# Batch 0's queries and keys loaded by fours, the weights' low parts on one engine, and new issue costs in a planner

## The chip, the cores and the metric

The kernel runs on one core of a Trainium2 chip. A core has a matrix engine (TensorE, PE in the profile), a vector engine (VectorE, DVE), an activation engine (ScalarE, ACT), a general engine (GpSimd, POOL) and a sync engine (SyncE, SP), which here issues every DMA. 16 DMA engines carry out what SP issues. The metric is the time of one execution on the device in microseconds, the median of the runs.

## What is computed

The input is q, k and v of 8 batches, 8 heads, 576 tokens and 64 elements, all float32, and weights of one feed-forward block. Cut to what matters:

```
factor, Sd = 4, S // 4
q_d, k_d, v_d = mean of each 4 tokens of q, k, v           # 144 pooled tokens
out_up    = repeat(softmax(q_d k_d^T / 8) v_d, 4)          # coarse attention
scores    = q k^T / 8, kept where |i - j| < 4              # local attention
out_local = softmax(scores) v
x   = out_up + out_local, heads side by side               # 4608 tokens x 512
xn  = (x - mean) / sqrt(var + 1e-6) * g_ln
out = x + relu(xn @ w_ch1) @ w_ch2                         # 512 -> 2048 -> 512
```

The weights arrive as float64 and are cut to float32 on the chip from their two 32-bit words. Each product of the feed-forward block is made of three matmuls, high by low, low by high and high by high, so each weight and each activation exists as a high part and a low part.

## The kernel before, in words

**The order is planned ahead.** Every step is given to a planner (`Plan`) with an engine, a cost in microseconds, its predecessors, a due time, the buffers that it takes and gives back, and for a DMA a latency (`lag`) and a size (`kb`). The planner walks through time, gives each engine the step that can start first and is due earliest, and the instructions are recorded in that order. On the chip each engine works its list strictly in that order. The costs are used for the order alone. `T0` and `CHUNK` set when the feed-forward chunks are due, `rate` the speed at which the planner lets DMAs land. A step can have a second engine (`alt`), and then the planner takes the one that can start first.

**Stages.** Local attention works in windows of 2 x 58 tokens, five per batch: `local(i)`. Coarse attention works by batch and by half of the heads: `pooled_half`. `norm(n)` joins both for a tile of 128 tokens and normalises it. `ffn(c, p)` is one of eight pairs of hidden blocks for chunk c of 256 tokens; there are 18 chunks. `weights(which, f)` loads one of the 32 blocks of weights and splits it. Chunks 0 and 1 run side by side while the weights come in; from chunk 2 on, all the weights are in the on-chip memory.

**Batch 0 before.** For each of its five windows, `load_rows` (L428) loads q and k with one token in a partition: two DMAs of 64 rows for each, each row in 8 pieces of 256 bytes, one for each head. `turn` (L458) transposes the block on PE with an identity matrix, four transposes of 128 x 128; `turn_out` (L465) copies the result from PSUM by ACT; `sums` (L480) adds four neighbouring tokens on DVE, four instructions for each block, which gives the pooled q and k of batch 0 (`gsum`). The scores (L526) use the turned blocks. The pooled scores of batch 0 (L766) need the sums of all windows. V comes behind q and k in SP's list: for the coarse attention in blocks of 72 rows with four tokens each (L700, `raw0v` and `raw1v`, 1024-byte pieces, added up on POOL at L713 and L714), and for the windows (L443, `vwin`). Behind V stand the first weights (L347, `s`).

**Weights.** ACT makes the high word (L359, `high_word`), DVE shifts and joins the low word (L367 and L370, `low_word`), ACT rounds to the high part (L378, `high`), and the low part is a subtraction (L383, `low`) for which the planner may choose DVE or POOL.

**Other steps named below.** `exps_by_pair` (L566) and `turn_a_out` (L582) are local attention's exponentials and the copy of the turned result; `times_v` (L596) multiplies by v; `turn_a_out` (L795) and `times_v` (L802, `gv`) are the same in the coarse attention; `expand` (L884, L890) joins the two for batch 0 on PE; `move` (L659, L662, `x<-xl`) copies rows of a window's result to the tile they belong to by DMA, at most 58 rows at a time. L197 is a matmul that only keeps PE busy. SP uses eight completion semaphores in turn: a DMA waits until the one eight places ahead of it has landed.

Of the kernel before, what the change touches and what calls it, by code (L numbers as in the profile page):

```python
# [22 lines left out]
class Plan:  # L23
# [3 lines left out]
    def __init__(self, rooms, spare):  # L27


        self.tasks = []  # L30
        self.rooms = rooms
        self.spare = spare
        self.cold = 3
        self.hold = 0.5
        self.lags = (80, 0.3, 0.6)
        self.rate, self.moved = 245.0, 0.0

# [102 lines left out]
def attention_then_ffn(  # L140
# [10 lines left out]
    nc = tc.nc  # L151
# [118 lines left out]

    T0 = 35
    C1 = 5
    CHUNK = 55
    PACE = CHUNK / NPR

# [43 lines left out]
    U, A, STG = (("u", 1),), (("a", 1),), (("stg", 1),)  # L319
    DMA, LAT, W_AHEAD = 0.5, 2.9, 40  # L320
# [16 lines left out]
    def weights(which, f):  # L337
# [42 lines left out]
        def low(eng):  # L380
            x = box[key]
            lo = unit([P, 512], f"lo{name}", F32R)
            eng.tensor_sub(lo, x.a.bitcast(F32), x.hi.bitcast(F32))  # L383
# [18 lines left out]
    chosen, own_moves = {}, []  # L402
    last_local = SimpleNamespace(v=[None] * NVW)

    def local(i):
# [44 lines left out]
        own = b < NPB  # L450
        for src, nm in ((q, "q"), (k, "k")):
            if by_pe:
# [14 lines left out]

                def sums(nm=nm):

                    for par in range(2):  # L470
                        t0 = window_start(w, par)
                        g0, g1 = (-(-(NQ * (2 * w + p)) // FACTOR) for p in (par, par + 1))
                        g1 = min(g1, SD)
                        c0 = 64 * par + FACTOR * g0 - t0
                        p = x.p[nm].rearrange("p (c t) -> p c t", c=NPAIR)
                        for hg in range(2):
                            key = (b, hg, nm)
                            if key not in gsum:
                                gsum[key] = unit([P, 2, SD], f"gs{nm}{b}_{hg}")
                            nc.vector.tensor_reduce(  # L480
                                out=gsum[key][:, :, g0:g1],
                                in_=p[:, 2 * hg : 2 * hg + 2, c0 : c0 + FACTOR * (g1 - g0)]
                                .rearrange("p c (g r) -> p c g r", r=FACTOR),
                                axis=AX.X, op=ALU.add,
                            )
# [4 lines left out]
                if own:  # L490
                    t = add("DVE", 4 * dve(120), sums, [t] + gsum_done.get((b, nm), []), due - 8.0,
                            take=() if w else (("u", 2),))
                    gsum_done.setdefault((b, nm), []).append(t)
                turned.append(add("ACT", act(512), turn_out, (t,), due - 8.0, take=U, give=A))
            else:
# [9 lines left out]
                for jb in range(2):  # L505
                    ts.append(add("SP", 4 * DMA, lambda src=src, nm=nm, jb=jb: load_blocks(src, nm, jb), ts,
                                  due - 14.0, take=() if jb else U, lag=LAT, kb=128, ahead=AHEAD))
                turned.append(add("DVE", dve(512), turn, ts, due - 8.0, take=U, give=U))
        vt = add("SP", 4 * DMA, load_v, (last_local.v[i % NVW],), due - 8.0, lag=LAT, kb=256, ahead=AHEAD)

        def scores_by_pair():

            x.ps = [
                psa(f"ls{i}_{h2}")[:, : NPAIR * 64].rearrange("p (c j) -> p c j", c=NPAIR) for h2 in range(2)
            ]
            for h2 in range(2):
                nc.tensor.matmul(
                    x.ps[h2], lhsT=ident_b, rhs=mask_b.unsqueeze(1).broadcast_to([P, NPAIR, 64]),
                    start=True, stop=False,
                )  # L520
            for pr in range(NPAIR):
                for h2 in range(2):
                    ds = slice(64 * h2, 64 * h2 + 64)
                    for par in range(2):
                        hs = slice(64 * par, 64 * par + 64)
                        nc.tensor.matmul(  # L526
                            x.ps[h2][hs, pr], lhsT=x.qt[ds, pr, hs], rhs=x.kt[ds, pr, hs],
                            start=False, stop=pr == NPAIR - 1,
                        )
# [76 lines left out]
        def divided(h2, eng):  # L606
# [7 lines left out]
            for pr in range(NPAIR):  # L614
# [3 lines left out]
        t = add("PE", 0.75, scores_by_pair if by_pe else scores_by_block, turned, due - 6.0,  # L618
                take=(("a", 2),), give=(("u", 2),))
        if not by_pe:  # L620
# [30 lines left out]
        for e, (n, p0, r0, m, par) in enumerate(moves):  # L651

            def move(n=n, p0=p0, r0=r0, m=m, par=par):
# [7 lines left out]
                for h2 in range(2):  # L661
# [4 lines left out]

            t = add("SP", DMA if by_pe else 2 * DMA, move, outs, due + 1.0, take=() if n in piece else U,
                    give=U if e == len(moves) - 1 else (), lag=LAT, kb=116)
# [13 lines left out]
    def pooled_half(b, hg):  # L682
# [6 lines left out]
        if own:  # L689
            ready["q"], ready["k"] = gsum_done[b, "q"], gsum_done[b, "k"]  # L690
        for nm, src in (("v", v),) if own else (("q", q), ("k", k), ("v", v)):
            for half in range(2):
# [34 lines left out]
    def pooled_pair(b, hg, pr, x, ready):  # L727
# [128 lines left out]
    def norm(n):  # L856
# [259 lines left out]
```

## Time and profile before

| | |
|---|---|
| median of 3 runs | 1064.73 us (1063.45 to 1066.62) |
| the profiled execution's own time | 1069.35 us |
| its span | 1067.0 us |
| busy: PE, DVE, ACT, POOL | 97%, 48%, 29%, 25% |
| DMA | 104.33 MB, mean 98 GB/s |

The profile's busy shares are means over stages that differ. The feed-forward of the first two chunks starts near 62 us, the weights are complete near 162 us, and after that PE is nearly always busy. A start row of the profile tells the time from the span's start, then the duration; "idle before" names what ended a wait. A row of the DMA view is cut into 40 equal slices of its window.

### The profile page before, as it was taken

To read this page: it belongs to the slowest core of one execution; us is meant where nothing else is said; L and a number is where in the kernel's file an instruction comes from. 1 tells how busy PE (TensorE), PEld (TensorE's weight loads), DVE (VectorE), ACT (ScalarE), POOL (GpSimd) and SP (SyncE) were. 2 spreads that over 40 slices of the span, in tenths; PEclk is the share of its full clock that TensorE was granted. 3 is DMA by queue.
4 is the path that set the end of the run, shared out by engine and by line. 5 is a ranking of instruction groups with operands and counts; after the bars stand their busy time and mean duration, and the time that the engine had idled before them with its cause. 6 is when DMAs were issued, how large, how long until landed. Compare 5 with 4: busy or idle time off the path is not lost.

```text
span 1067.0 us, 23720 instructions
## 1 busy us (share of the span) xinstructions
PE 1039.3 (97%) x9280; PEld 932.2 (87%) x9280; DVE 509.5 (48%) x1307; ACT 313.2 (29%) x856; POOL 268.7 (25%) x286
## 2 busy tenths in 40 slices
PE   8897899989999999999999999999989999999998
PEld 8786789979999888889898989898989989888997
DVE  7589954634353534444444443545434454534211
ACT  5575632413332222132222221223222222222110
POOL 4233546323105221231224150142301400000000
PEclk9898999999999999999999999999999999999999
DMA  7788445535433533344354434243442443201000
GB/s 156 214 230 287 129 106 123 146 80 114 88 86 82 119 82 92 69 94 97 77 118 95 106 78 114 42 130 74 109 90 66 87 87 76 62 27 32 9 20 20
DMA packets 289295, 104.33 MB, mean 98 GB/s; under 512 B 237945, under 2 KB 276089, under 8 KB 289185
## 3 DMA queue, kind: packets, MB, share of 16 engines
q1 hardware_dynamic: 289185, 102.83, 40.7%
q8 instruction: 73, 1.20, 0.5%
q14 instruction: 37, 0.30, 0.1%
HBM read 82.58 MB, written 11.80 MB: 88 GB/s over the span
## 4 chain that ended last, share of the span: by engine, by line
PE 87%; DMA 4%; DVE 4%; SPq 2%; ACT 1%; issue 1%; POOL 0%; DVEq 0%; ACTq 0%; POOLq 0%
PE h L996 36%; PE acc L1019 35%; PE gv L802 3%; DMA s<-in_moe_w_ch_dram 3%; PE lv L596 2%; PE gs L766 2%; PE ls L540 2%; PE lt L575 1%; PE px L923 1%; PE gt L785 1%; SPq L428 1%; DVE cva L370 1%; DMA x<-xl 1%; PE gq L739 1%; DVE lo L383 1%
## 5 line engine op out<-in xcount | busy, mean ns | idle before, releaser
L1019 PE MATMUL acc<-hi,hl 128*128 128x512 f32 x576 | 238.2, 413 | 5.3 <-DVE hl L1007 5.3
L1019 PE MATMUL acc<-lo,hh 128*128 128x512 f32 x576 | 228.2, 396 | 0.0
L1019 PE MATMUL acc<-hi,hh 128*128 128x512 f32 x576 | 226.2, 393 | 0.0
L1003 ACT ACTIVATE hh<-h 128x512 fp32r<-128x512 f32 x144 | 86.2, 599 | 437.8 <-PE h L996 393.6
L1007 DVE SCALAR_TENSOR_TENSOR hl<-h,hh 128x512 fp32r<-128x512 f32 x144 | 98.9, 687 | 222.3 <-ACT hh L1003 214.7
L996 PE MATMUL h<-xh,lo 128*128 128x256 f32 x1152 | 193.2, 290 | 0.0
L996 PE MATMUL h<-xlo,hi 128*128 128x256 f32 x1152 | 185.3, 283 | 0.0
L996 PE MATMUL h<-xh,hi 128*128 128x256 f32 x1152 | 185.1, 283 | 0.0
L996 PEld LDWEIGHTS h<-xh,lo 128*128 128x128 f32 x1152 | 168.4, 190 | 16.9 <-POOL lo L383 0.2
L996 PEld LDWEIGHTS h<-xlo,hi 128*128 128x128 f32 x1152 | 159.1, 192 | 0.0
L996 PEld LDWEIGHTS h<-xh,hi 128*128 128x128 f32 x1152 | 158.6, 191 | 0.0
L896 POOL TENSOR_TENSOR x<-x,up 128x512 f32<-128x512 f32 x32 | 41.2, 1289 | 416.6 <-DMA x<-xl 310.9
L1019 PEld LDWEIGHTS acc<-hi,hh 128*128 128x128 f32 x576 | 109.0, 189 | 25.3
L1019 PEld LDWEIGHTS acc<-hi,hl 128*128 128x128 f32 x576 | 109.8, 191 | 22.0 <-DVE hl L1007 6.4
L1019 PEld LDWEIGHTS acc<-lo,hh 128*128 128x128 f32 x576 | 109.9, 191 | 12.5
L930 ACT ACTIVATE xh<-px,gain 128x128 fp32r<-128x128 f32 x144 | 43.6, 372 | 77.1 <-PE px L923 47.7
L940 DVE SCALAR_TENSOR_TENSOR xlo<-px,gain,xh 128x128 fp32r<-128x128 f32 x144 | 42.7, 344 | 34.7 <-ACT xh L930 34.5
L904 DVE BATCH_NORM_STATS2 st<-x 128x6 f32<-128x512 f32 x32 | 21.9, 686 | 47.1 <-POOL x L896 46.0
L779 ACT ACTIVATE ag<-gs,gmx 96x144 f32<-96x144 f32 x96 | 28.9, 373 | 42.9 <-DVE gmx L771 42.7
L1027 DVE SCALAR_TENSOR_TENSOR x<-acc,x 128x512 f32<-128x512 f32 x36 | 24.4, 688 | 35.3 <-PE acc L1019 35.3
L546 DVE TENSOR_TENSOR ls<-ls,mask 128x256 f32<-128x256 f32 x66 | 26.6, 424 | 27.2 <-PE ls L540 27.2
L802 PEld LDWEIGHTS gv<-vd,agt 72*72 72x72 f32 x512 | 37.2, 145 | 1.4
(191 smaller groups left out, 1156.8 us busy)
## 6 DMA issues: line engine op xcount, KB each, us to landing
s<-in_moe_w_ch_dram SPq DMA_DIRECT2D x64, 256.0 KB
vwin<-in_v_dram SPq DMA_DIRECT2D x160, 64.0 KB
out_dram<-x SPq DMA_DIRECT2D x36, 256.0 KB
qr<-in_q_dram SPq DMA_DIRECT2D x264, 32.0 KB
kr<-in_k_dram SPq DMA_DIRECT2D x264, 32.0 KB
up<-ud SPq DMA_DIRECT2D x28, 256.0 KB
x<-xl SPq DMA_DIRECT2D x66, 58.0 KB
ud<-od SPq DMA_DIRECT2D x32, 72.0 KB
```

The lines of the kernel that those rows point to most:

```text
L546: nc.vector.tensor_add(x.ps[n], x.ps[n], mask.unsqueeze(1).broadcast_to([P, NPAIR, 64]))
L779: nc.scalar.activation(y.a[:, c], y.ps[:, c], AF.Exp, scale=POOLED_SCALE, bias=y.mx[:, c : c + 1])
L802: nc.tensor.matmul(y.pv[:, qh, h2], lhsT=y.at[kh][:, h2, qh * GH : (qh + 1) * GH], rhs=vd[:, kh, 2 * pr + h2], start=kh == 0, stop=kh == 1,)
L896: nc.gpsimd.tensor_add(xt[n], xt[n], x.up)
L904: nc.vector.bn_stats(st, x.up if by_pe else xt[n])
L930: nc.scalar.activation(xh[c][i][:, k, j * P : (j + 1) * P], pxt[n][:, kc], AF.Copy, scale=gain[:, kc : kc + 1])
L940: nc.vector.scalar_tensor_tensor(out=xlo[c][i][:, k, ts], in0=pxt[n][:, kc], scalar=gain[:, kc : kc + 1], in1=xh[c][i][:, k, ts].bitcast(F ...
L996: nc.tensor.matmul(ph[c, p][:, fi], lhsT=wt[:, kc], rhs=xx[kc // 2][:, kc % 2], start=n == 0, stop=n == 3 * KC - 1)
L1003: nc.scalar.activation(hh[c, p], ph[c, p], AF.Relu)
L1007: nc.vector.scalar_tensor_tensor(out=hl[c, p].rearrange("p c t -> p (c t)"), in0=ph[c, p].rearrange("p c t -> p (c t)"), scalar=0.0, in1=h ...
L1019: nc.tensor.matmul(acc[c][j], lhsT=lt[:, fi, ts], rhs=rt, start=p == 0 and fi == 0 and n == 0, stop=p == NPR - 1 and fi == 1 and n == 2,)
L1027: nc.vector.scalar_tensor_tensor(out=x, in0=acc[c][j], scalar=1.0 + 2.0**-23, in1=x, op0=ALU.mult, op1=ALU.add)
```

## The change

**Batch 0.** The new `own_half` replaces the loads, turns and sums of batch 0's five windows. The pooled tokens 0 to 73 are half 0, and 71 to 143 are half 1. For each half, each of q and k and each pair of heads there is one DMA (L419) that puts four neighbouring tokens, 1024 contiguous bytes, in a partition: 74 partitions by 2 heads in half 0, 73 by 2 in half 1, 16 DMAs in all where there were 20. PE turns a block with eight matmuls (L428) that each have 64 columns of the block as the stationary operand and the identity as the moving one, and writes each to the place of every fourth token, so the tokens stand in order. DVE adds fours with one instruction for each block (L438), ACT copies out (L445), and the windows' scores (L570) take their 64 tokens from the half that holds them.

**Low parts.** `low` has no second engine any more: all 32 are on DVE.

**Planner.** Costs of SP's steps and of the weights' steps, the latency (2.9 to 2.5, for weights 4.0), `rate` 245 to 260, `T0` 35 to 30 and `CHUNK` 55 to 56.

```diff
-    T0 = 35
+    T0 = 30
     C1 = 5
-    CHUNK = 55
+    CHUNK = 56
...
-        t = add("SP", 2 * DMA, load, (), due, take=(("u", 3),), lag=LAT, kb=512, ahead=W_AHEAD)
-        t = add("ACT", 2 * act(256, True), high_word, (t,), due)
-        t = add("DVE", 0.45 + 2 * dve(256), low_word, (t,), due, give=(("u", 2),))
+        t = add("SP", 1.3, load, (), due, take=(("u", 3),), lag=LAT + W_LAG, kb=512, ahead=W_AHEAD)
+        t = add("ACT", 0.87, high_word, (t,), due)
+        t = add("DVE", 1.26, low_word, (t,), due, give=(("u", 2),))
         t = add("ACT", act(512, True), high, (t,), due, take=U)
-        return add("DVE", dve(512), lambda: low(nc.vector), (t,), due, take=U, give=U,
-                   alt=("POOL", pool(512), lambda: low(nc.gpsimd), 0.3))
+        return add("DVE", 0.69, lambda: low(nc.vector), (t,), due, take=U, give=U)
...
+    own_t, own_done = {}, {}
+    OWN_G = ((0, GH + 2), (GH - 1, SD))
+
+    def own_half(b, half):
+        g0, g1 = OWN_G[half]
+        ng = g1 - g0
...
+            def load(x=x, nm=nm, src=src, pr=pr):
+                x.raw = unit([P, 2, FACTOR, D], f"{nm}o{b}_{pr}_{half}")[:ng]
+                nc.sync.dma_start(
+                    x.raw.rearrange("p h r d -> p h (r d)"),
+                    src[b, 2 * pr : 2 * pr + 2, FACTOR * g0 : FACTOR * g1].rearrange("h (g r) d -> g h (r d)", r=FACTOR),
+                )
+
+            def turn(x=x, nm=nm, pr=pr):
+                x.p = psa(f"l{nm}{b}_{pr}_{half}")[:, : FACTOR * ng].rearrange("p (g r) -> p g r", r=FACTOR)
+                for r in range(FACTOR):
+                    for h2 in range(2):
+                        nc.tensor.matmul(
+                            x.p[64 * h2 : 64 * h2 + 64, :, r], lhsT=x.raw[:, h2, r], rhs=ident[:ng, :ng],
+                            start=True, stop=True,
+                        )
...
-        for src, nm in ((q, "q"), (k, "k")):
+        for src, nm in () if own else ((q, "q"), (k, "k")):
...
-                t = add("SP", 1.46, lambda src=src, nm=nm: load_rows(src, nm), (), due - 12.0, take=U,
-                        lag=LAT, kb=256, ahead=AHEAD)
+                t = add("SP", 1.33, lambda src=src, nm=nm: load_rows(src, nm), (), due - 12.0, take=U,
+                        lag=LAT, kb=360, ahead=AHEAD)
```

**SP, from the last loads of q and k to the first weights.** Before (`qn`, `kn` are q and k of a window, x2 its two halves; `raw0v`, `raw1v` and `vwin` are V; `s` is weights):

```order
L428 DMA qn_272<-in_q_dram 64x8x64 x2
L428 DMA kn_309<-in_k_dram 64x8x64 x2
L700 DMA raw0v_332<-in_v_dram 72x4x256
L700 DMA raw1v_361<-in_v_dram 72x4x256
L443 DMA vwin_76<-in_v_dram 64x4x64 x4
L443 DMA vwin_77<-in_v_dram 64x4x64 x4
L700 DMA raw0v_458<-in_v_dram 72x4x256
L443 DMA vwin_78<-in_v_dram 64x4x64 x4
L700 DMA raw1v_504<-in_v_dram 72x4x256
L443 DMA vwin_79<-in_v_dram 64x4x64 x4
L347 DMA s_0_0_546<-in_moe_w_ch_dram 128x2x256
```

Now, the same stretch with the semaphores that each row waits for (`qo` and `ko` are the new blocks; DMAHW0 to DMAHW7 are the eight completion semaphores):

```order
L419 DMA ko_2_0_164<-in_k_dram 74x2x256 [waits DMAHW0_49]
L419 DMA qo_1_1_179<-in_q_dram 73x2x256 [waits DMAHW1_49]
L419 DMA ko_1_1_194<-in_k_dram 73x2x256 [waits DMAHW2_49]
L419 DMA qo_3_0_208<-in_q_dram 74x2x256 [waits DMAHW3_49]
L419 DMA ko_3_0_222<-in_k_dram 74x2x256 [waits DMAHW4_49]
L419 DMA qo_2_1_236<-in_q_dram 73x2x256 [waits DMAHW5_49]
L419 DMA ko_2_1_248<-in_k_dram 73x2x256 [waits DMAHW6_49]
L419 DMA qo_3_1_267<-in_q_dram 73x2x256 [waits DMAHW7_49]
L419 DMA ko_3_1_282<-in_k_dram 73x2x256 [waits DMAHW0_49]
L746 DMA raw0v_298<-in_v_dram 72x4x256 [waits DMAHW1_49]
L746 DMA raw0v_310<-in_v_dram 72x4x256 [waits DMAHW2_49]
L499 DMA vwin_76<-in_v_dram 64x4x64 [waits DMAHW3_49,DVE_49]
```

V and the weights follow in nearly the same order; the blocks ahead of them have 74 or 73 rows where they had 64.

**DVE, the sums and the windows.** Before, the sums of a window's q and k stand next to the maxima of the window ahead (`gsq`, `gsk` sums, `lmx` maxima of the scores `ls`):

```order
L480 TENSOR_REDUCE gsk_0_178<-lk_206 128x2x14
L480 TENSOR_REDUCE gsk_1_180<-lk_206 128x2x14
L551 TENSOR_REDUCE lmx_252<-ls_0_220 128x4
L551 TENSOR_REDUCE lmx_252<-ls_1_221 128x4
L556 TENSOR_TENSOR ls_0_220<-ls_0_220,lmx_252 128x256
L556 TENSOR_TENSOR ls_1_221<-ls_1_221,lmx_252 128x256
L480 TENSOR_REDUCE gsq_0_158<-lq_244 128x2x15
```

Now:

```order
L438 TENSOR_REDUCE gsk_1_278<-lk_2_1_340 128x72
L438 TENSOR_REDUCE gsq_1_259<-lq_3_1_377 128x72
L438 TENSOR_REDUCE gsk_1_278<-lk_3_1_388 128x72
L595 TENSOR_REDUCE lmx_415<-ls_0_352 128x4
L595 TENSOR_REDUCE lmx_415<-ls_1_353 128x4
L600 TENSOR_TENSOR ls_0_352<-ls_0_352,lmx_415 128x256
L600 TENSOR_TENSOR ls_1_353<-ls_1_353,lmx_415 128x256
L816 TENSOR_REDUCE gmx_0_448<-gs_0_406 96x3
```

All 16 sums stand ahead of the first window's maxima; the last of them is that of `ko_3_1`, the last load.

**POOL, low parts.** Before, a stretch of POOL's list in the weights' stage (`lo` low parts, `raw2q` to `kd` the coarse sums of batch 1):

```order
L383 TENSOR_TENSOR lo_3_1342<-cva_3_956,hi_3_1317 128x512
L713 TENSOR_TENSOR raw2q_1129<-raw2q_1129 72x4x128
L714 TENSOR_TENSOR qd_1371<-raw2q_1129 72x256
L713 TENSOR_TENSOR raw2k_1133<-raw2k_1133 72x4x128
L714 TENSOR_TENSOR kd_1410<-raw2k_1133 72x256
L383 TENSOR_TENSOR lo_4_1438<-cva_4_1182,hi_4_1415 128x512
L383 TENSOR_TENSOR lo_4_1477<-cva_4_1319,hi_4_1464 128x512
```

Now:

```order
L956 TENSOR_TENSOR mv_1059<-mv_1059,neg_half 128x1
L759 TENSOR_TENSOR raw2q_1248<-raw2q_1248 72x4x128
L760 TENSOR_TENSOR qd_1384<-raw2q_1248 72x256
L759 TENSOR_TENSOR raw2k_1261<-raw2k_1261 72x4x128
L760 TENSOR_TENSOR kd_1420<-raw2k_1261 72x256
L759 TENSOR_TENSOR raw2q_1442<-raw2q_1442 72x4x128
L760 TENSOR_TENSOR qd_1384<-raw2q_1442 72x256
```

14 low parts left POOL for DVE; the coarse sums stay.

More of the change, by code (lines that the diff above doesn't have):

```diff
@@ L35, in __init__ @@
         self.lags = (80, 0.3, 0.6)
-        self.rate, self.moved = 245.0, 0.0
+        self.rate, self.moved = 260.0, 0.0
     def add(self, eng, dur, fn, deps=(), due=0.0, take=(), give=(), lag=None, ahead=1e9, alt=None, kb=0):
@@ L319, in attention_then_ffn @@
     U, A, STG = (("u", 1),), (("a", 1),), (("stg", 1),)
-    DMA, LAT, W_AHEAD = 0.5, 2.9, 40
+    DMA, LAT, W_AHEAD, W_LAG = 0.5, 2.5, 40, 1.5
     def act(n, sbuf=False):
@@ L402, in attention_then_ffn, with sums, turn_out @@
     chosen, own_moves = {}, []
-    last_local = SimpleNamespace(v=[None] * NVW)
+    own_t, own_done = {}, {}
[3 more added lines that the diff above has]
+        ng = g1 - g0
+        add = plan.add
+        for e, (nm, src, pr) in enumerate((nm, src, pr) for pr in range(NPAIR) for nm, src in (("q", q), ("k", k))):
+            due = window_at(b * NWIN + (2 * half if half else 0)) - 8.0 + 0.2 * e
+            x = SimpleNamespace()
+            def load(x=x, nm=nm, src=src, pr=pr):
[12 more added lines that the diff above has]
+                        )
+            def sums(x=x, nm=nm, pr=pr):
+                key = (b, pr // 2, nm)
+                if key not in gsum:
+                    gsum[key] = unit([P, 2, SD], f"gs{nm}{b}_{pr // 2}")
+                n0 = half * GH - g0
+                nc.vector.tensor_reduce(
+                    out=gsum[key][:, pr % 2, half * GH : (half + 1) * GH], in_=x.p[:, n0 : n0 + GH], axis=AX.X, op=ALU.add
+                )
+            def turn_out(x=x, nm=nm, pr=pr):
+                t = unit([P, 512], f"o{nm}t{b}_{pr}_{half}")
+                own_t[nm, pr, half] = t
+                nc.scalar.copy(t[:, : FACTOR * ng], x.p.rearrange("p g r -> p (g r)"))
+            t = add("SP", 0.5, load, (), due - 4.0, take=U, lag=LAT, kb=147, ahead=AHEAD)
+            t = add("PE", 0.45, turn, (t,), due, take=A, give=U)
+            done = gsum_done.setdefault((b, pr // 2, nm), [])
+            done.append(add("DVE", dve(288), sums, [t] + done, due + 1.0, take=() if half or pr % 2 else U))
+            own_done.setdefault((b, half), []).append(add("ACT", act(296), turn_out, (t,), due, take=U, give=A))
@@ L405, in local, with own_piece @@
+    def own_piece(nm, pr, w, par, ds):
+        t0 = window_start(w, par)
+        half = int(t0 + 64 > FACTOR * OWN_G[0][1])
+        t0 -= FACTOR * OWN_G[half][0]
+        return own_t[nm, pr, half][ds, t0 : t0 + 64]
+    last_local = SimpleNamespace(v=[None] * NVW, ls=None)
     def local(i):
@@ L466, in turn_out @@
                     setattr(x, nm + "t", t)
[L468 to L485, printed above, removed]
-                t = add("SP", 1.46, lambda src=src, nm=nm: load_rows(src, nm), (), due - 12.0, take=U,
-                        lag=LAT, kb=256, ahead=AHEAD)
+                t = add("SP", 1.33, lambda src=src, nm=nm: load_rows(src, nm), (), due - 12.0, take=U,
+                        lag=LAT, kb=360, ahead=AHEAD)
                 t = add("PE", 0.43, turn, (t,), due - 8.0, take=A, give=U)
[L490 to L493, printed above, removed]
                 turned.append(add("ACT", act(512), turn_out, (t,), due - 8.0, take=U, give=A))
@@ L506, in local @@
                     ts.append(add("SP", 4 * DMA, lambda src=src, nm=nm, jb=jb: load_blocks(src, nm, jb), ts,
-                                  due - 14.0, take=() if jb else U, lag=LAT, kb=128, ahead=AHEAD))
+                                  due - 14.0, take=() if jb else U, lag=LAT, kb=200, ahead=AHEAD))
                 turned.append(add("DVE", dve(512), turn, ts, due - 8.0, take=U, give=U))
-        vt = add("SP", 4 * DMA, load_v, (last_local.v[i % NVW],), due - 8.0, lag=LAT, kb=256, ahead=AHEAD)
+        if own:
+            for half in range(2):
+                if half in {int(window_start(w, par) + 64 > FACTOR * OWN_G[0][1]) for par in range(2)}:
+                    turned += own_done[b, half]
+            turned.append(last_local.ls)
+        vt = add("SP", 2.65 if own else 2.65, load_v, (last_local.v[i % NVW],), due - 8.0, lag=LAT, kb=360, ahead=AHEAD)
         def scores_by_pair():
@@ L520, in scores_by_pair, with of @@
                 )
+            def of(nm, pr, par, ds):
+                if own:
+                    return own_piece(nm, pr, w, par, ds)
+                return getattr(x, nm + "t")[ds, pr, 64 * par : 64 * par + 64]
             for pr in range(NPAIR):
@@ L618, in local @@
         t = add("PE", 0.75, scores_by_pair if by_pe else scores_by_block, turned, due - 6.0,
-                take=(("a", 2),), give=(("u", 2),))
+                take=(("a", 2),), give=() if own and w not in (2, NWIN - 1) else (("u", 2 * NPAIR if own else 2),))
+        if own:
+            last_local.ls = t
         if not by_pe:
@@ L665, in move @@
                     )
-            t = add("SP", DMA if by_pe else 2 * DMA, move, outs, due + 1.0, take=() if n in piece else U,
+            t = add("SP", 0.76 if by_pe else 2.0, move, outs, due + 1.0, take=() if n in piece else U,
                     give=U if e == len(moves) - 1 else (), lag=LAT, kb=116)
@@ L716, in pooled_half @@
                 by_dve = b == 0 and nm == "k"
-                t = add("SP", 0.82, load, (), due - 4.0, take=STG, lag=LAT, kb=288, ahead=AHEAD)
+                t = add("SP", 0.45, load, (), due - 4.0, take=STG, lag=LAT, kb=288, ahead=AHEAD)
                 t = add(
@@ L849, in pooled_pair @@
         od_done.append(t)
-        t = add("SP", DMA, keep, (t,), due, lag=LAT)
+        t = add("SP", 0.42, keep, (t,), due, lag=LAT)
         ud_done.setdefault(b, []).append(t)
@@ L962, in norm @@
         else:
-            t = add("SP", DMA * len(rows), load_up, [d for _, _, b, _ in rows for d in ud_done[b]], due - 4.0,
+            t = add("SP", 0.64 * len(rows), load_up, [d for _, _, b, _ in rows for d in ud_done[b]], due - 4.0,
                     take=U, lag=LAT, kb=256, ahead=12.0)
@@ L1061, in attention_then_ffn @@
     spread_done = plan.add("POOL", 2.5, make_spread, (choice_done,), 20.0, take=U)
+    for b in range(NPB):
+        for half in range(2):
+            own_half(b, half)
     for i in range(NPB * NWIN):
```

4 lines of the change are left out of this document (2 added, 2 removed).

## The prediction

> **What bounds the kernel now.** I read the busy time by stages first, from the page and the view by windows (columns: busy us of PE, weight load, DVE, ACT and POOL, granted clock, DMA share, GB/s).
>
> ```profile
> span 1067.0 us, 23720 instructions
> ...
> 0.00:20.00 20.00, 17.63 (x212) 15.87 (x216) 15.07 (x58) 9.04 (x18) 8.43 (x28) 1.00 0.70 158
> 20.00:40.00 20.00, 19.60 (x317) 17.79 (x318) 13.05 (x49) 15.82 (x55) 7.92 (x8) 1.00 0.73 167
> 40.00:60.00 20.00, 16.80 (x134) 14.04 (x132) 10.69 (x33) 8.87 (x24) 3.48 (x5) 0.83 0.91 265
> 80.00:140.00 60.00, 47.92 (x348) 40.63 (x347) 55.83 (x101) 35.33 (x92) 28.61 (x24) 0.94 0.63 187
> 160.00:1000.00 840.00, 834.20 (x7549) 751.35 (x7549) 374.48 (x981) 212.94 (x588) 203.81 (x208) 1.00 0.39 87
> ```
>
> From 160 us on PE idles 5.8 us in 840: nothing of this change shortens that work, so the end moves by as much as its beginning moves. From 80 to 140 DVE is the fullest engine, 55.83 of 60 us, and PE idles 12.1. Ahead of that lies batch 0's attention, a chain with no second batch to hide behind. What ends last there is seen in SP's list, PE's list and the chain of waits.
>
> ```profile
> 1.31 1.43 SPq L428 DMA_DIRECT2D qn<-in_q_dram  x2
> ...
> 13.63 2.02 SPq L428 DMA_DIRECT2D kn<-in_k_dram  x2
> 15.70 0.64 SPq L700 DMA_DIRECT2D raw0v<-in_v_dram  x1
> ...
> 23.89 2.57 SPq L443 DMA_DIRECT2D vwin<-in_v_dram  x4
> 26.56 0.51 SPq L700 DMA_DIRECT2D raw1v<-in_v_dram  x1
> 27.17 3.05 SPq L443 DMA_DIRECT2D vwin<-in_v_dram  x4
> 30.26 3.27 SPq L347 DMA_DIRECT2D s<-in_moe_w_ch_dram  x4
> ```
>
> ```profile
> 5.50 0.45 PE L458 MATMUL lq<-ident,qn 128*128 128x128 f32 x1 [0.23 <-DMA qn<-in_q_dram]
> ...
> 19.15 0.63 PE L458 MATMUL lk<-ident,kn 128*128 128x128 f32 x4 [0.27 <-DMA kn<-in_k_dram]
> ```
>
> ```profile
> 32.71 4.32 PE gv L802 x64
> ```
>
> The last k is issued by 15.65 and used at 19.15; the coarse attention's product with v follows at 32.71, and the first weights are issued at 30.26 behind all of V. Both start from the moment at which q and k are through. The question is when that is in the changed kernel.
>
> **How many engines a load gets.** The new loads have 74 and 73 rows, so I looked for loads with odd numbers of rows. At 790 us only copies of 58 and 46 rows are in flight (the SP row shows six copies issued back to back; then their sizes, 1 KB a row, the two of 12 rows taken to be through by 791; then three windows).
>
> ```profile
> 786.46 5.95 SPq L662 DMA_DIRECT2D x<-xl  x6
> ```
>
> ```profile
> x<-xl SPq DMA_DIRECT2D x2, 58.0 KB
> x<-xl SPq DMA_DIRECT2D x2, 46.0 KB
> x<-xl SPq DMA_DIRECT2D x2, 12.0 KB
> ```
>
> ```profile
> 791.00:792.00 1.00, 1.00 (x6) 0.76 (x5) 0.91 (x3) 0.00 (x0) 0.00 (x0) 1.00 0.16 36
> 792.00:793.00 1.00, 1.00 (x11) 1.00 (x10) 0.12 (x1) 0.00 (x0) 0.55 (x1) 1.00 0.16 36
> 793.00:794.00 1.00, 1.00 (x10) 0.99 (x9) 0.00 (x0) 0.00 (x0) 0.00 (x0) 1.00 0.16 36
> ```
>
> The share stands still at 0.16 with several copies waiting: 2 of 16 engines are 0.125, and packets that overlap count a little more. So 58 rows (2 x 29) and 46 rows (2 x 23) got two engines each, and the same two, or the share would be higher. A load of 72 rows by 4 heads in pieces of 1024 bytes, alone on the queue:
>
> ```profile
> 621.12 0.31 SPq L700 DMA_DIRECT2D raw12q<-in_q_dram  x1
> ```
>
> ```profile
> DMA  0899100012942345588878987877775412210000
> GB/s 0 36 36 53 53 18 0 36 36 89 71 89 71 107 125 178 196 267 285 303 249 303 321 285 267 303 267 267 267 178 107 89 36 53 53 36 0 0 0 0
> ```
>
> Its plateau is 7 to 8 tenths and mostly 267 GB/s: 12 of 16 engines, and 72 = 12 x 6. All three counts are the largest divisor of the rows that is at most 16. By that pattern 74 = 2 x 37 gets two engines and 73, a prime, one. No row shows a load on one engine; that step is the pattern carried on.
>
> The Trainium skill has it as a rule, in "DMA: Bandwidth & Descriptors", section "Why a DMA increments its semaphore by 16 and not by 1": the count is the largest k up to 16 that divides the slowest dimension of both sides, and a DMA issued from SP takes the lowest-numbered k engines. The trace's 58, 46 and 72 rows agree. By it the one-engine loads also sit on one of the two engines of the 74-row loads.
>
> **The change, part by part.** *Loads.* A 74-row load is 148 pieces of 1024 bytes, 74 on each of two engines; a 73-row load is 146 on one. There are eight of each. With all on the same pair, as the copies above were, the busier engine has 8 x 74 + 8 x 146 = 1760 pieces. Its rate: 267 GB/s over 12 engines is 22.3 GB/s, 46 ns a piece. That is 1760 x 0.046 = 81.0 us. Bounds: the plateau's best slice, 321 / 12 = 26.8 GB/s, gives 38 ns and 67 us; two engines at 36 GB/s, scaled by bytes, 57 ns and 100 us. I take 46, the same size of piece from the same memory. The first DMAs were issued by 2.74 and used at 5.50, 2.8 us, of which some 0.6 is their own transfer. So the last k is used at about 1.3 + 0.4 (one issue; 0.31 to 0.64 in the rows above) + 2.2 + 81.0 = 84.9, against 19.15: 65.8 later.
>
> *What is queued behind.* V and the weights stand behind these loads in SP's list, and each waits for the DMA eight places ahead. Eight DMAs of V are issued while the blocks land and have their share behind them on the busy engine; 13 remain ahead of the first weight, 11 for the windows and two for the coarse attention, which also wait until POOL has added up the first two blocks. 11 x 0.64 (2.57 for four) + 2 x 0.5 = 8.0 us, and some 1.7 for POOL: the weights start at 94.5 instead of 30.26, 64 later. On the compute side every sum stands ahead of the first window's maxima in DVE's list, so four windows and the coarse scores run after 85 one behind the other; the coarse product then ends near 101, against 37, again 64. I take 64 for both.
>
> *Turns.* PE's price for eight matmuls of 64 x 74 is not in the trace. Below: four transposes of 128 x 128 take 0.63, and eight of the 64 x 64 products on all four corners of the array less, by the chain of waits:
>
> ```profile
> 20.00 0.62 PE ls L526 x32
> ```
>
> Above: 64 records of 72 x 65 take 4.32, so 16 for one turn 1.1. At 0.45 (the first transposes' row) to 1.1, sixteen turns are 7 to 18 us, but a load lands every 3.4 to 6.7 us, and that covers all but the last turn. The same cover hides the ACT copies and the sums. If the loads were quick, PE would pay (rivals).
>
> *Low parts.* The rows of the instructions, and one pair on POOL and DVE:
>
> ```profile
> L383 DVE TENSOR_TENSOR lo<-cva,hi x18: 676/684/1359, 71.5 to 161.2; 128x512 fp32r<-128x512 f32 x18
> L383 POOL TENSOR_TENSOR lo<-cva,hi x14: 1275/1296/1558, 47.4 to 124.1; 128x512 fp32r<-128x512 f32 x14
> ...
> L367 DVE TENSOR_SCALAR cva<-cva x32: 410/421/1524, 39.3 to 146.6; 128x512 int32<-128x512 int32 x32
> ```
>
> ```profile
> 100.91 1.55 POOL L383 TENSOR_TENSOR lo<-cva,hi 128x512 fp32r<-128x512 f32 x1 [2.41 <-ACT hi L378]
> ```
>
> ```profile
> 101.23 1.52 DVE L367 TENSOR_SCALAR cva<-cva 128x512 int32<-128x512 int32 x1
> ```
>
> DVE gains 14 x 0.68 = 9.6 us of work in the stage where it is the fullest engine. But beside POOL's 1.55 us the shift took 1.52 instead of 0.42: 1.1 us lost. If each of the 14 costs DVE between 0 and 1.1, the balance is +9.6 to -5.8; most POOL low parts lie in that stage, where DVE is 93% busy, so some 0.6 each is likely, and I take +1. PE's 12.1 us idle in that stage is also the most that the new costs, due times and order of the planner can return; a late weight can cost as much. I take 0, 3 either way.
>
> *Clock.* PE waits some 60 us with only the turns; between 40 and 60, after shorter waits, the granted clock was 0.83, 3.4 us in 20. I add 1 us for a cold restart.
>
> **Sum.** 64 + 1 + 0 + 1 = 66, less 1 for V that has already landed: +65. The profiled execution took 1069.35 and would become 1134. It is 4.6 above the median of the runs, 1064.73, to which the same 65 gives **1130**.
>
> **Rivals.** *One-engine loads elsewhere* (8%): if 73 rows use a third engine, it has 8 x 146 = 1168 pieces, 53.7 us; the last k is used at 57.6, 38 later, and the time is about 1102. For it: no row shows which engine a single one is. Against: the copies all shared one pair.
>
> *Sixteen engines after all* (5%, faster): if pieces are dealt out whatever the rows, 16 loads are 2368 x 0.046 / 16 = 6.8 us. SP's 16 issues then bind at about 0.5 each, and the last k is used near 12, 7 ahead of before, so 1058. It decides from the point where the busiest engine needs no more than before's 15 us: 330 pieces, about 21 a load, seven engines. Against: 116 KB in two copies at 36 GB/s.
>
> *Quick loads, slow turns* (3%, no change): with sixteen engines and turns of 1.1 us, PE is the bound from 4 us on, 16 x 1.1 = 17.6, and q and k are through at 21.6 against 19.8: 1066. The two halves of a block go to different columns of the array, and the row of `ls` shows such columns side by side at 0.62 us for 32 records, so 0.5 is as possible.
>
> **How the numbers follow.** 84% for the forecast. Its own range comes from the piece: 38 to 57 ns are -14 to +19, the other terms 4; without the far ends 1112 to 1144, which leaves the first rival out. Slower by over 0.3% (3.2 us, about what this kernel's runs can tell from none): 92% with the first rival; within: 3%; faster: 5%.
>
> **What would show it.** In the changed profile: DMA share near 0.1 and some 25 to 45 GB/s from 10 to 80 us; SP's `ko` and `qo` rows spread over some 35 us with waits; PE's turns 3.4 and 6.7 us apart, the last near 85; first weights issued near 94; low parts on DVE at 0.68 and the shift near 0.42; PE dense from about 225. Wrong it is if the share is high in the first 15 us, if the last turn comes ahead of 30, or if the stage after the first weights is shorter or longer by more than 5 us than before's.

## The result: 1115.23 us, slower by 50

The changed kernel took 1115.23 us (median of 4 runs, 1114.15 to 1116.16) against 1065.29 for the kernel before (4 runs, 1063.45 to 1066.62); the ratio is 1.0456, with a 95% interval of 1.0434 to 1.0478. The forecast was 1130 in a range of 1112 to 1144: the direction and the cause hold, the size is 15 us too large. The profiled executions span 1112.4 and 1067.0 us, 45.4 apart; the execution of before that was profiled (1069.35) stood 4.1 us above the median of these runs, the changed kernel's 1.1 below.

SP's list in the changed kernel, which answers to the loads of q and k quoted ahead of the result (start, duration):

```profile
1.31 0.40 SPq L419 DMA_DIRECT2D qo<-in_q_dram  x1
1.76 0.45 SPq L419 DMA_DIRECT2D ko<-in_k_dram  x1
2.25 3.24 SPq L419 DMA_DIRECT2D qo<-in_q_dram  x1
5.52 3.30 SPq L419 DMA_DIRECT2D ko<-in_k_dram  x1
...
61.34 6.02 SPq L419 DMA_DIRECT2D ko<-in_k_dram  x1
67.41 7.35 SPq L746 DMA_DIRECT2D raw0v<-in_v_dram  x2
...
89.94 2.14 SPq L347 DMA_DIRECT2D s<-in_moe_w_ch_dram  x4
```

PE's list, with the idle time before each turn in brackets:

```profile
7.75 1.25 PE L428 MATMUL lq<-ident,qo 74*64 74x74 f32 x16 [2.46 <-DMA qo<-in_q_dram]
10.89 1.25 PE L428 MATMUL lk<-ident,ko 74*64 74x74 f32 x16 [1.89 <-DMA ko<-in_k_dram]
...
23.08 1.24 PE L428 MATMUL lq<-ident,qo 73*64 73x73 f32 x16 [4.67 <-DMA qo<-in_q_dram]
29.39 1.24 PE L428 MATMUL lk<-ident,ko 73*64 73x73 f32 x16 [5.07 <-DMA ko<-in_k_dram]
...
80.13 1.24 PE L428 MATMUL lk<-ident,ko 73*64 73x73 f32 x16 [6.04 <-DMA ko<-in_k_dram]
...
97.20 1.38 PE L848 MATMUL gv<-vd,agt 72*72 72x65 f32 x18
98.93 3.20 PE L848 MATMUL gv<-vd,agt 72*72 72x65 f32 x46 [0.35 <-issue]
```

A load of 74 rows adds 3.14 us to the time of its turn and one of 73 rows 6.2 to 6.3 (the last 7.3). With 74 and 146 pieces on the busier engine that is 42 to 43 ns a piece in both. The view of the DMA engines from 5 to 67 us, cut into 40 slices, shows the engines themselves:

```profile
GB/s 48 48 48 48 48 48 48 39 24 24 24 24 37 36 48 48 48 36 24 24 24 24 24 24 31 36 48 43 48 36 24 24 24 24 24 24 24 24 24 24
```

48 GB/s is two engines, 24 is one (1024 bytes in 42.7 ns). Nowhere is it more than 48: no load has a third engine. That holds also from 26.7 to 29.4 us, while a load of 73 rows is still landing (its turn stands at 29.39) and the next one of 74 has begun: a single engine outside the pair would make it 72 there. The trace's records of the completion semaphores agree: as the data of a load of 74 rows land, two increments come, and one for a load of 73 rows (one more stands right behind the issue, at 1.82 us for the first load).

So the last k is used at 80.13 instead of 19.15, the first weights are issued at 89.94 instead of 30.26 (59.7 later), and the coarse product stands at 97.20 instead of 32.71 (64.5 later). From the first weights on the changed kernel is quicker, though. Two windows of each, the 130 us from its first weights and what follows up to 1030 (width, then busy us of PE, weight load, DVE, ACT and POOL, granted clock, DMA share, GB/s), before first, then changed:

```profile
30.30:160.30 130.00, 114.63 (x1029) 99.83 (x1020) 102.96 (x232) 74.33 (x205) 50.87 (x45) 0.95 0.69 194
160.30:1030.00 869.70, 863.90 (x7738) 778.28 (x7737) 381.17 (x996) 218.10 (x601) 203.51 (x208) 1.00 0.38 85
```

```profile
89.90:219.90 130.00, 123.85 (x1184) 111.53 (x1184) 110.40 (x255) 80.35 (x226) 45.72 (x43) 0.97 0.73 205
219.90:1030.00 810.10, 807.46 (x7361) 725.78 (x7362) 374.88 (x971) 207.68 (x567) 188.66 (x194) 1.00 0.39 88
```

PE idles 15.4 us in the first 130 before and 6.2 after the change, then 5.8 and 2.6. That is 12.4 us of the 14.3 by which the span grew less than the first weights moved (59.7 - 45.4). The first product of the feed-forward, before and then changed, moved by nearly the same:

```profile
62.12 0.72 PE L996 MATMUL h<-xh,lo 128*128 128x256 f32 x4
```

```profile
121.35 0.71 PE L1042 MATMUL h<-xh,lo 128*128 128x256 f32 x4
```

It stands 59.2 us later, 5.3 less than the coarse product, and the span from it to the end is 13.8 shorter. So the changed kernel wins time both ahead of the feed-forward and in it. This is the part that the forecast had at 0. The profiled execution of before took 4.1 us more than its median, so these differences of spans are too large by about as much; the runs below give them by medians.

### The profile page after: what moved, and what is told of

Its sections match the earlier page's. It is cut to its first block, busy times and chain, and to the rows that moved or that the text cites. A ratio compares the mean times of both kernels' runs of the same rounds, so it can differ in the third digit from the quotient of the medians.

```text
span 1112.4 us, 23962 instructions
## 1 busy us (share of the span) xinstructions
PE 1043.8 (94%) x9450; PEld 936.5 (84%) x9450; DVE 519.4 (47%) x1300; ACT 311.8 (28%) x850; POOL 250.6 (23%) x272
## 4 chain that ended last, share of the span: by engine, by line
PE 81%; SPq 6%; DVE 5%; DMA 5%; issue 1%; POOL 0%; ACT 0%; DVEq 0%; ACTq 0%; POOLq 0%
PE h L1042 34%; PE acc L1065 33%; SPq L419 5%; PE gv L848 3%; PE gs L812 2%; DMA s<-in_moe_w_ch_dram 2%; PE lv L640 2%; PE ls L584 2%; DMA ko<-in_k_dram 2%; DVE cva L370 2%; PE lt L619 1%; DVE lo L383 1%; PE px L969 1%; PE gt L831 1%; DVE cva L367 1%
## 5 line engine op out<-in xcount | busy, mean ns | idle before, releaser
L1065 PEld LDWEIGHTS acc<-lo,hh 128*128 128x128 f32 x576 | 109.2, 190 | 12.4
L956 POOL TENSOR_TENSOR mv<-mv,neg_half 128x1 f32<-128x1 f32 x36 | 20.0, 556 | 99.4 <-DVE mv L953 78.0
L848 PE MATMUL gv<-vd,agt 72*72 72x65 f32 x512 | 38.2, 228 | 0.3 <-issue 0.3
```

Source lines behind the costliest of these rows:

```text
L848: nc.tensor.matmul(y.pv[:, qh, h2], lhsT=y.at[kh][:, h2, qh * GH : (qh + 1) * GH], rhs=vd[:, kh, 2 * pr + h2], start=kh == 0, stop=kh == 1,)
L1065: nc.tensor.matmul(acc[c][j], lhsT=lt[:, fi, ts], rhs=rt, start=p == 0 and fi == 0 and n == 0, stop=p == NPR - 1 and fi == 1 and n == 2,)
```

## Experiments: the rows of a load

All kernels here differ from the changed kernel in one line; no instruction changes its place, only its number of rows.

```diff
-    OWN_G = ((0, GH + 2), (GH - 1, SD))      # 74 and 73 rows
+    OWN_G = ((0, GH + 8), (GH - 8, SD))      # 80 and 80; GH + 2, GH - 2: 74; + 3, - 3: 75; + 4, - 4: 76
```

**80 and 80 rows.**

> Both halves have 80 pooled tokens (0 to 79 and 64 to 143) instead of 74 and 73; the order of all instructions is the changed kernel's. Theory (the largest divisor of the rows up to 16 sets the engines): 80 rows get 16 engines, the share of the first 15 us is 0.6 or more instead of 0.12, SP issues the 16 loads without a wait in about 7 us, and the turns stand back to back on PE: 16 at the 1.25 us that one took in the changed kernel are 20 us, so the last k is turned near 25 us instead of 81, and the first weights are issued near 24 instead of 89.9. The time falls by 56 to 66 us from 1115: 1049 to 1059. Rival (the rows don't matter, the slow part is the form of the load with four tokens in a partition): the turns stay 3 to 6 us apart and the time stays over 1100.

Measured: 1047.45 us (6 runs, 1043.58 to 1055.76) against 1065.08 for before; ratio 0.9832 (0.9791 to 0.9873). PE's and SP's lists:

```profile
5.21 0.79 PE L428 MATMUL lq<-ident,qo 80*64 80x80 f32 x16
5.84 0.72 PE L428 MATMUL lk<-ident,ko 80*64 80x80 f32 x16
...
16.13 0.72 PE L428 MATMUL lk<-ident,ko 80*64 80x80 f32 x16
...
29.96 4.37 PE L848 MATMUL gv<-vd,agt 72*72 72x65 f32 x64
```

```profile
9.46 0.31 SPq L419 DMA_DIRECT2D ko<-in_k_dram  x1
...
26.73 2.94 SPq L347 DMA_DIRECT2D s<-in_moe_w_ch_dram  x4
```

More bytes, and 68 us less: the rows alone cost that much. The turns were quicker than expected: some 0.6 us apart, so the last is done at 16.9 and not near 25, and the time fell by 2 us more than the range given.

**74 and 74 rows.**

> Both halves have 74 rows (0 to 73 and 70 to 143); nothing else differs from the changed kernel. Theory: all 16 loads get two engines, 148 pieces of 42 ns on two, so a turn every 3.1 us, the last near 5 + 50 = 55 us instead of 80, and about 1090. Rival (the pace of 3.1 and 6.2 us comes from the wait for the eighth DMA back or from something else than the count of engines): the second half's loads still land 6 us apart and the time stays near 1115.

Measured: 1086.03 us (one run). The turns in PE's list:

```profile
7.06 1.25 PE L428 MATMUL lq<-ident,qo 74*64 74x74 f32 x16 [1.78 <-DMA qo<-in_q_dram]
10.21 1.26 PE L428 MATMUL lk<-ident,ko 74*64 74x74 f32 x16 [1.89 <-DMA ko<-in_k_dram]
...
55.34 1.25 PE L428 MATMUL lk<-ident,ko 74*64 74x74 f32 x16 [2.73 <-DMA ko<-in_k_dram]
```

3.14 us apart but for the last two (3.4 and 4.0), the last at 55.3: one more row in the second half saves 29 us. The pace follows the count of engines.

**75 and 75 rows, then 76 and 76.**

> Both halves have 75 rows (0 to 74 and 69 to 143), one row more than the larger half of the changed kernel. Theory: 75 = 5 x 15, so 15 engines, and within 3 us of the 80-row kernel. Rival (any count that isn't a multiple of 16, or an odd one, is slow): like 74 rows or slower, 1090 or more.

> Both halves have 76 rows (0 to 75 and 68 to 143). The largest divisor up to 16 is 4 (76 = 4 x 19): 16 loads of 152 pieces on four engines are 608 pieces each at 42 ns, 25.5 us, a turn every 1.6 us, the last near 31 instead of 16.1 with 80 rows and 80.1 in the changed kernel; about 1061. Rival (more rows are simply better between 74 and 80, as 75 rows look): as fast as 75 rows, under 1054.

Measured: 75 rows 1052.72 us, 76 rows 1063.95 (one run each). In PE's list of the 76-row kernel the turns stand 1.62 us apart, 38 pieces of 42.6 ns on each of four engines:

```profile
7.38 0.75 PE L428 MATMUL lk<-ident,ko 76*64 76x76 f32 x16 [1.01 <-DMA ko<-in_k_dram]
9.00 1.28 PE L428 MATMUL lq<-ident,qo 76*64 76x76 f32 x16 [0.88 <-DMA qo<-in_q_dram]
...
31.70 1.28 PE L428 MATMUL lk<-ident,ko 76*64 76x76 f32 x16 [0.68 <-DMA ko<-in_k_dram]
```

So 74, 75, 76 and 80 rows give 1086, 1053, 1064 and 1047: not by size but by the divisor (2, 15, 4, 16). The Trainium skill states that rule in "DMA: Bandwidth & Descriptors", section "Why a DMA increments its semaphore by 16 and not by 1": the largest divisor of the slowest dimension up to 16, on the lowest-numbered engines. The five counts measured here agree, and so does the one-engine load, which shared an engine with the two-engine ones. For 75 rows, where no spacing shows the count, the completion semaphores do: 15 increments come as a load's data land, 4 with 76 rows and 16 with 80. The one run of the 75-row kernel is 5 us slower than the 80-row one, more than the 3 expected. Its DMAs are not the reason: no turn waits for one, and SP issues the first weights even 1.4 us sooner (25.34 against 26.73). The turns themselves are slow, and so is everything on PE until some 28 us:

```profile
5.21 1.27 PE L428 MATMUL lq<-ident,qo 75*64 75x75 f32 x16
6.26 1.21 PE L428 MATMUL lk<-ident,ko 75*64 75x75 f32 x16
...
22.07 1.22 PE L428 MATMUL lk<-ident,ko 75*64 75x75 f32 x16
23.21 3.20 PE L812 MATMUL gs<-gsk,qbdg 128*96 128x144 f32 x12
...
27.73 1.71 PE L812 MATMUL gs<-gsk,qbdg 128*96 128x144 f32 x12
...
38.43 4.37 PE L848 MATMUL gv<-vd,agt 72*72 72x65 f32 x64
```

```profile
25.34 2.15 SPq L347 DMA_DIRECT2D s<-in_moe_w_ch_dram  x4
```

The two rows of L812 are the same instructions at 3.20 and at 1.71 us: TensorE ran at about half its pace. The coarse product stands at 38.43 instead of 29.96, 8.5 later, and the span is 6.4 longer (1051.0 against 1044.6) although the weights came sooner. So in this pair the chain through the coarse product set the time, not the queue up to the weights.

**75 rows again.**

> The 75-row kernel once more, to see whether its turns stand 1.0 us apart again (the profiled execution had them at 1.21 us each, until 27 us, and the 80-row one at 0.72 to 0.78). Theory (16 turns of 64 columns don't keep TensorE's clock up by themselves; it depends on whether the first matmuls, ahead of them, have brought it up): either pace, and with the quick one 1046 to 1049, with the slow one 1050 to 1054. Rival (15 engines or 75 partitions are slower by themselves): 1052 to 1055 and turns at 1.2 us again with every profile.

Measured: 1049.07 us (4 runs: 1052.83, 1046.88, 1050.20, 1047.94), ratio to before 0.9851 (0.9821 to 0.9882). The profiled execution was the slowest, and its turns were slow again, as in the first profile. All four lie within the range of the 80-row kernel's runs (1043.58 to 1055.76), so the 5 us are not clear of noise. Slow turns go with 1052.7 and 1052.8, but whether the turns of the 1046.88 were quick isn't shown, so neither reading is ruled out.

## Experiments: the low parts and the planner's numbers

The time won outside batch 0's loads has to come from the rest of the change. The first question was which half.

**80 rows, low parts on two engines.** The 80-row kernel, with this in `low`:

```diff
-        return add("DVE", 0.69, lambda: low(nc.vector), (t,), due, take=U, give=U)
+        return add("DVE", 0.69, lambda: low(nc.vector), (t,), due, take=U, give=U,
+                   alt=("POOL", pool(512), lambda: low(nc.gpsimd), 0.3))
```

> 80 rows as in the run above, and the low parts may go to POOL again as in the kernel before. Theory (as in the prediction: what DVE gains by fewer low parts it loses to POOL's port): within 4 us of the 80-row kernel. Rival (the 12 us less idle time on PE after the first weights, 8.8 us instead of 21, came from the low parts on DVE): 8 to 14 us slower than the 80-row kernel.

Measured: 1058.35 us (12 runs), 10.9 more than the 80-row kernel on the same chip. The theory of the prediction falls. Its arithmetic holds: the groups of DVE's weight rows in the 130 us from the first weights, first with POOL, then on DVE alone (count, then busy us and mean ns of one):

```profile
L370 DVE SCALAR_TENSOR_TENSOR cva<-s,cva 128x256 int32<-128x256 int32 x64 | 40.4, 672 | 1.1
L367 DVE TENSOR_SCALAR cva<-cva 128x512 int32<-128x512 int32 x32 | 19.9, 622 | 0.0
L383 DVE TENSOR_TENSOR lo<-cva,hi 128x512 fp32r<-128x512 f32 x17 | 12.6, 748 | 0.0
```

```profile
L370 DVE SCALAR_TENSOR_TENSOR cva<-s,cva 128x256 int32<-128x256 int32 x62 | 33.2, 576 | 1.1
L383 DVE TENSOR_TENSOR lo<-cva,hi 128x512 fp32r<-128x512 f32 x29 | 24.2, 846 | 0.2 <-ACT hi L378 0.2
L367 DVE TENSOR_SCALAR cva<-cva 128x512 int32<-128x512 int32 x31 | 17.1, 550 | 2.1 <-ACT cva L359 2.1
```

12 more low parts on DVE cost 11.6 us there and the other rows gave 10.0 back (three instructions fewer among them): DVE's work is nearly the same, 72.9 and 74.5 us. The 11 us lie elsewhere. Next, the two edits on the kernel before, one at a time and together.

```diff
 before, low parts on DVE
-        return add("DVE", dve(512), lambda: low(nc.vector), (t,), due, take=U, give=U,
-                   alt=("POOL", pool(512), lambda: low(nc.gpsimd), 0.3))
+        return add("DVE", dve(512), lambda: low(nc.vector), (t,), due, take=U, give=U)
 before, new numbers
-        self.rate, self.moved = 245.0, 0.0
+        self.rate, self.moved = 260.0, 0.0
-    T0 = 35
+    T0 = 30
-    CHUNK = 55
+    CHUNK = 56
-    DMA, LAT, W_AHEAD = 0.5, 2.9, 40
+    DMA, LAT, W_AHEAD, W_LAG = 0.5, 2.5, 40, 1.5
...
```

> The kernel before with all low parts on DVE and nothing else. Theory (the 11 us between the two 80-row kernels come from where the low parts run): 8 to 13 us faster than before, 1052 to 1057. Rival (they come only with the planner's new numbers): within 4 us of before.

> The kernel before with the planner's new numbers (T0, CHUNK, rate, latencies, costs of SP's and the weights' steps); loads and low parts as before. Theory (where the low parts run decides): within 4 us of before, 1061 to 1069. Rival (the numbers decide): 8 us or more faster.

> The kernel before with the new numbers and all low parts on DVE: the change without the new loads. In the 80-row kernel the last k is turned 3 us earlier than before and the first weights are issued 3.5 us earlier; if that is what the new loads are worth, this kernel takes 3 to 4 us more than the 80-row kernel's 1047.5, 1050 to 1052. If the new loads are worth nothing it takes 1047; if they carry most of the gain over before (17.6 us), 1058 or more.

> The 80-row kernel (new loads, low parts on DVE) with the planner's numbers of before. Theory (the numbers are worth at most 4 us either way): 1044 to 1052. Rival (the numbers carry the gain): 1056 or more.

| loads of batch 0 | planner's numbers | low parts | us (runs) | ratio to before (95%) |
|---|---|---|---|---|
| as before | old | DVE | 1072.74 (4) | 1.0070 (1.0042 to 1.0098) |
| as before | new | DVE and POOL | 1064.09 (10) | 0.9987 (0.9968 to 1.0006) |
| as before | new | DVE | 1050.61 (4) | 0.9863 (0.9834 to 0.9892) |
| 80 rows | old | DVE | 1074.33 (4) | 1.0109 (1.0053 to 1.0165) |
| 80 rows | new | DVE and POOL | 1058.35 (12) | 0.9937 (0.9911 to 0.9962) |
| 80 rows | new | DVE | 1047.45 (6) | 0.9832 (0.9791 to 0.9873) |

The first theory (the low parts alone gain 8 to 13 us) and the last (the numbers are worth at most 4) fall. Of the two between, the numbers came true, in the first of them not for its reason, that the low parts alone decide. The low parts on DVE alone are 7.6 us slower, the numbers alone change nothing, and both together give 14.6 us. With 80 rows the numbers are worth 26.9 us. The third row is the change without its loads, so the loads of 74 and 73 rows cost 1115.23 - 1050.61 = 64.6 us. Done with 80 rows they are worth 3.2 us by the medians; the two kernels' intervals overlap, so that gain isn't separated from nothing. The table has the same comparison twice more: with the old numbers the 80-row loads lose 1.6 us, and with low parts on both engines they gain 5.7, where the intervals don't overlap. So what the loads are worth depends on the rest of the lists. The windows, from the first weights on, of the first three kernels of the table:

```profile
29.70:159.70 130.00, 115.50 (x1065) 100.87 (x1062) 104.93 (x252) 75.53 (x209) 33.28 (x34) 0.96 0.69 196
159.70:1030.00 870.30, 861.90 (x7694) 775.34 (x7693) 378.15 (x988) 216.40 (x596) 200.81 (x206) 0.99 0.37 85
```

```profile
29.70:159.70 130.00, 118.73 (x1113) 105.82 (x1113) 106.54 (x238) 77.48 (x213) 58.35 (x52) 0.97 0.75 204
159.70:1030.00 870.30, 863.78 (x7694) 775.60 (x7693) 381.50 (x992) 212.59 (x579) 198.86 (x203) 0.99 0.37 83
```

```profile
29.00:159.00 130.00, 122.92 (x1135) 108.17 (x1134) 110.79 (x249) 75.89 (x212) 46.66 (x44) 0.99 0.78 210
159.00:1030.00 871.00, 869.41 (x7759) 782.47 (x7758) 383.41 (x998) 216.01 (x586) 190.20 (x194) 1.00 0.37 82
```

PE's idle time in the two windows is 14.5 and 8.4, then 11.3 and 6.5, then 7.1 and 1.6 us. In the first kernel ACT stands for weights that haven't landed, by the view of its waits (total us, times, longest):

```profile
ACT cva L359 <- DMA s<-in_moe_w_ch_dram: 16.5, 10, 5.0
```

**Which numbers.** The old ones have a weight's work on DVE at 1.11 + 0.60 us and its landing 2.9 us behind the issue; the measured DVE work, by the medians of its rows, is 0.42 + 2 x 0.42 + 0.68 = 1.94. So the next two kernels divide the numbers, on the kernel before with the low parts on DVE.

```diff
 weights' numbers only
-        t = add("SP", 2 * DMA, load, (), due, take=(("u", 3),), lag=LAT, kb=512, ahead=W_AHEAD)
-        t = add("ACT", 2 * act(256, True), high_word, (t,), due)
-        t = add("DVE", 0.45 + 2 * dve(256), low_word, (t,), due, give=(("u", 2),))
+        t = add("SP", 1.3, load, (), due, take=(("u", 3),), lag=4.0, kb=512, ahead=W_AHEAD)
+        t = add("ACT", 0.87, high_word, (t,), due)
+        t = add("DVE", 1.26, low_word, (t,), due, give=(("u", 2),))
...
```

> The kernel before with all low parts on DVE (1072.7 us alone) and, of the planner's new numbers, only those of the weights' steps: SP 1.3, latency 4.0 instead of 2.9, ACT 0.87, DVE 1.26 and 0.69. Theory (with the old numbers the planner puts DVE's and ACT's weight steps ahead of weights that haven't landed: ACT waited 16.5 us for them, DVE 5.1 us behind ACT): these numbers bring back most of the 22 us, 1050 to 1058. Rival (due times, rate or the other SP costs carry it): 1066 or more.

> The kernel before with all low parts on DVE and all new numbers except those of the weights' steps, which keep 1.0, 2.9, 0.67, 1.11 and 0.60. Theory: 1066 to 1075, as with the old numbers. Rival (due times, rate or the other SP costs carry it): 1050 to 1058. If both kernels of this pair lie between, the two groups share it.

Measured: 1076.10 us with the weights' numbers only (4 runs, ratio 1.0114, 1.0080 to 1.0148), 1062.27 with the others only (10 runs, 0.9979, 0.9957 to 1.0001). With neither it was 1072.74, with both 1050.61. The theory falls again, and the other numbers alone bring back 10.5 of the 22 us, short of what the rival asked for. The weights' numbers gain only on top of the others (11.7 us). In the stage that they price they did what they should, and the time was lost later. ACT's wait for weights in the first of these two kernels, its two windows, and the waits of PE from 155 to 330 us:

```profile
ACT cva L359 <- DMA s<-in_moe_w_ch_dram: 7.6, 8, 2.5
```

```profile
29.90:159.90 130.00, 121.31 (x1107) 109.38 (x1098) 108.09 (x247) 76.85 (x216) 40.95 (x38) 0.95 0.73 206
159.90:1030.00 870.10, 852.28 (x7614) 766.04 (x7613) 376.37 (x989) 215.00 (x592) 195.87 (x200) 0.99 0.37 82
```

```profile
PE lt L574 <- ACT la L569: 6.9, 1, 6.9
PE px L922 <- DVE xn L913: 5.2, 1, 5.2
```

The wait for weights fell from 16.5 to 7.6 us and PE's idle time in the first window from 14.5 to 8.7, but in the second it is 17.8 instead of 8.4: an attention window and a norm of later batches come too late for PE. Those have their due times from `T0` and `CHUNK`, which this kernel keeps old. That the due times are what removes these two waits is likely but not shown by a run of its own, and neither is why the low parts on POOL take the gain away (their kernels' lists differ in many places).

## Why the prediction was right, and where its sizes were off

**Engines by divisor: right.** It is the step that carried the forecast, and the one without a row, a single engine for 73 rows on the same pair, is now a row: 24 GB/s. The rival of one-engine loads on a third engine is refuted by the same view (48 GB/s and not 72 where both kinds of load are under way), the two with sixteen engines by the spacing of the turns.

**Size of a piece: 46 ns taken, 42.5 measured.** The plateau of twelve engines was read low: its twelve slices of 249 to 321 GB/s average 282, which is 23.5 an engine and 43.6 ns, where the commonest slice, 267, was taken. With 42.5, 1760 pieces are 74.8 us, 6.2 less. The first turn came some 0.7 us later than this pace would have it and about as much went between the loads, so the last k came at 80.13 instead of 84.9.

**What is queued behind: right for the weights, too short for the compute side.** From the last k to the first weights it is 9.8 us (forecast 9.6), with 13 DMAs of V in between as forecast. The way there was not: SP never had eight of the loads out (last section), so it reached V only at 67.41. From the first use of the last k to the end of the coarse product it is 22.0 us, where 16 was taken. The loads came 4.8 sooner and this chain took 5.9 longer, so the product ended 65.1 later (102.13, against 37.0 before) where 64 was forecast: two errors that cancel, and that agreement is luck.

**Clock: 1 us taken, 2.5 to 3.3 seen.** TensorE was at half pace when the last k came: the first group of coarse scores took 3.19 us and the second, at 85.68, 1.71. From the last k to the start of the coarse product the 80-row kernel, at full pace from its first turn, needs 13.8 us, the 75-row one 16.4 and the changed one 17.1, with the same lists.

**Loads, in all: 64 taken (with +1 for the clock and -1 for V), 64.6 measured** between the medians of the kernels with and without them. The 1 us for V is not separated by any run.

**Low parts +1, the planner's numbers 0 within 3: together -14.6 by the medians.** This is the step that failed. The kernel with only these two edits takes 1050.61 us against 1065.18 before. DVE's balance near 0 was right as a sum of its work, and it didn't decide: with the old numbers the same move costs 7.6 us, with the new ones it gains 13.5 (1064.09 to 1050.61). The two edits were priced one by one, and the bound of 3 us on a reordered list came from no row: PE's idle 15.4 us from the first weights on, and 5.8 behind them, was there to be won and 12.4 of it was. The prediction named 12.1 of that idle time as the most that could come back, and still took 0. By its own last sign, a stage behind the first weights that is more than 5 us shorter, this part is refuted: it was 14.3 shorter. Why the two edits need each other stays open.

The sum then closes in the medians: +64.6 - 14.6 = +50.0, and 49.9 was measured.

**The range: 1115 lies in it by 3 us, and that is in part luck.** Its lower end came from a piece of 38 ns. The piece's true size lowers the time by 6, the longer chain behind it raises it by as much, and what took the time down by 15 was a term for which the range had 4.

**Turns: right.** They cost nothing in the changed kernel but for the last. At full pace they take 0.6 us each, within the bounds of 0.45 to 1.1; at half pace they stand 1.0 apart and last 1.21 to 1.28.

**The rival with sixteen engines** would have given 1047 and not 1058: the last k came at 16.13 and not 12, which is 3 us ahead of before and not 7, and the -14.6 was missing there too. With it the break-even against before lies near four engines (76 rows, 1063.95), not seven.

## What to carry to other kernels

Before choosing how many rows a load has, take the largest divisor up to 16: 73 rows and 74 rows cost 65 us here, and 80 rows, with 9% more bytes, nothing. A narrow load isn't only slow itself; it holds up everything behind it in the queue.

Price an edit of a planner's costs together with the other edits that change its lists, and take the idle time of the busiest engine in that stage as the bound of what it can return. Here neither edit gained alone and both together gained 1.4%.

## What the runs showed of the hardware that was not expected

**SP's issue itself stalls on narrow loads.** In the changed kernel the third load's instruction lasts 3.24 us instead of 0.40, and each later one about as long as a load takes to land; with 76 rows it is the fifth (at 3.12 us):

```profile
2.66 0.42 SPq L419 DMA_DIRECT2D ko<-in_k_dram  x1
3.12 1.98 SPq L419 DMA_DIRECT2D qo<-in_q_dram  x1
```

At that point 2 x 74 or 4 x 38 pieces, 148 or 152, had been issued to an engine. So the eight completion semaphores were not what limited SP. With 80 rows, ten pieces a load and engine, all sixteen went out at 0.31 to 0.49 us each. What the limit is was not tried.

**TensorE can stay at about half pace for 20 us of steady work.** The 75-row and the 80-row kernel begin with the same 16 filler matmuls from 1.50 us; the turns then follow without a gap at about half the pace in the one (22.07 still 1.22) and at full pace from the first in the other. The profile's granted clock reads 1.00 in both. In the 76-row kernel, where the turns go from 0.75 to 1.28 us at 9.00, it reads 0.50 from there to 25 us, though PE is 80% busy in that stretch; so the slow turns there go with half the clock, and the 1.00 of the 75-row kernel doesn't fit its rows. The Trainium skill, in "TensorE: Matmul & The Clock Gate", section "Part 1: The HAM clock gate (the "warmup" mystery)", has the array go to full pace after about 3.4 us of sustained work, with a window that isn't tied to the kernel's start. The 80-row kernel agrees; the 75-row kernel's two profiles don't, with 20 us and more. The quick pace came with the products over all 128 rows (L812, 3.20 and then 1.71); whether products of 75 rows by 64 columns are too little to bring it up was not tried.
